# Four more single steps, in half products over 64 rows, at the head of a fused MLP's forward and backward pass

## The chip, the cores and the metric

The kernel runs on one core of a Trainium2 chip. The time is the device time of one execution in microseconds (us); the median of several executions is what is compared. The engines are named as in the profile: PE (matrix products), PEld (PE's weight loads), DVE (vector engine), ACT (scalar engine), POOL and SP (here they issue transfers for the most part). Each engine works through its own queue in order, and waits for the others through semaphores.

## The reference

One MLP layer with a GELU, forward and backward, in bfloat16, for 2048 rows, D = 448 and F = 1792:

```python
h   = gelu_tanh(x @ w1 + b1)          # 2048 x 1792
out = h @ w2 + b2                     # 2048 x 448
# vjp with grad_out g:
gh  = (g @ w2.T) * gelu_tanh'(x @ w1 + b1)
gx  = gh @ w1.T ;  gw1 = x.T @ gh ;  gb1 = sum(gh)
gw2 = h.T @ g   ;  gb2 = sum(g)
```

Six results are returned: out, gx, gw1, gb1, gw2, gb2. In the kernel u stands for x @ w1 (transposed, F on the partitions), q for g @ w2.T.

## The kernel before

**Tiles.** The 2048 rows are cut into four blocks of 512 (NB). F is cut into 14 tiles of 128, taken two at a time: a *step* k is one block and one pair of F tiles, so there are 28 steps (NSTEP), seven to a block. For a step PE makes u (into two banks of PSUM, the accumulator memory) and q (into a two-bank tile). D = 448 is three times 128 and a rest of 64, so each of the two F tiles needs three products over 128 rows and a *tail* over 64 rows.

**Full and half products.** A product over 128 rows can also be made as two *half products* over 64 rows each, one on the lower and one on the upper rows of the array, side by side with another half product. `side_by_side(one, other)` issues such pairs: a low half of `one` with a high half of `other`. Each product goes into two banks in turn, so that no bank is written from both halves at once; `half_product` (L257) puts a wait of PE on itself where a bank changes its half. u of a step needs 6 pairs, q 6 pairs, and the tails of a u and a q go side by side (`pe_tail_pair`, `pe_tails`).

**Elementwise work of a step.** ACT copies u out of PSUM with its bias (`copy_u`, L346), squares it (`act_square`, L355), takes its gelu into hT (`act_gelu`, L352) and a tanh of a cubic that DVE prepares (`act_tanh`, L364). DVE makes the cubic (L383 and L385 for one step, L359 and L360 for two), the gate (L387 to L394, or L368 to L375), and last *gh*, the gradient (L400), which multiplies the gate with q out of PSUM and so frees q's bank. The areas are fixed: AZ for cubic and gate, U4 for the u of two steps.

**Units.** A *unit* is one output tile of 128 rows x 448: kind "o" is out = hT times w2, kind "x" is gx = ghT times w1T, each 14 products over the F tiles, or 28 half products. Two units go side by side (`units_side`): first one gets the low half of every F tile and the other the high half, then (second = True) the reverse. A finished unit is cast to bfloat16 by ACT (L441, kind "x" and the first block's "o") or by DVE (L443, the other "o"), and POOL issues its store. `evictions()` casts whatever is finished, at the place where it is called. The units come in the order o, x of block 0, o, x of block 1, and so on, four each.

**Single steps.** Steps 0 to 7 (NSINGLE = 8) run one by one: in step i, PE makes u of step f = i + 2 and q of step i, and between their sections pieces of units that fill the time in which a bank must not be touched. At the end of step i ACT has tanh i, the copies, square and gelu of f; DVE has one chain written out by name (`dve_chain`). The units of block 0's out run in steps 1 to 6, two x units in steps 6 and 7.

**Paired steps.** From then on two steps ks run together, with elementwise work over both: tanh over 2048 elements, a gate in five instructions with `evictions` in its midst, two gh. In the first three pairs (n <= 2) PE makes u in full products (`pe_u_fulls`, L242), in the first two also q (`pe_q_fulls`, L303) and one x unit each (`pieces`, L430). From the third pair on (k = 12 and 13) q and the next u are made side by side (`pe_q_rows`), and two o or x units run side by side in the midst of the next u.

**Banks.** Eight banks: four single (`one0` to `one3`) for u, and for units when free, and two double ones (`two0`, `two1`). A single step's q always uses `two0`; in pairs the even step uses `two0` and the odd one `two1`. `open_two(1, 2)` opens two units in `two1`. Single steps' u use `one0` and `one1`, pairs use all four.

**Order.** The program's order is each engine's order: nothing is reordered afterwards. `traffic(i)` issues, on SP, the transposed copies of gh and the loads of the next blocks' x and g; `stores(n, fmax)` issues n stores of h. After the 28 steps the rest of the units, and then gw1 and gw2 are made (from 154 us on in the profiled execution).

Of the kernel before, what the change touches and what calls it, by code (L numbers as in the profile page):

```python
# [11 lines left out]
BF16 = mybir.dt.bfloat16  # L12
# [7 lines left out]
def kernel(  # L20
# [15 lines left out]
    nc = tc.nc  # L36
    P = 128
# [9 lines left out]
    SPB = SB // P  # L47
    NPAIR = NF // 2
    NSTEP = NB * NPAIR
    NSINGLE = 8  # L50
    LEAD = 2
    NWAKE = 10
    STG = 5
# [140 lines left out]
    PU, PQ = {}, {}  # L194
    order_a, order_b = [0, 1, 2, 3], [0, 1]
    U4 = tmp.tile([P, 4, SB], BF16, name="U4", tag="U4", bufs=1)
    SETS = [8, 4]

    def cols(p, a):
        return slice((2 * FP[p] + a) * P, (2 * FP[p] + a + 1) * P)  # L200
# [4 lines left out]
    def place(first, ks):  # L205
        return AZ[:, first:first + 2 * len(ks), :]
# [4 lines left out]

    def part_z(ks):
        k = ks[0]
        return place(4 * (k % 3) + 2 if k < NSINGLE else 2 * (k % 2), ks)

    def runs(ks):
        out = []
# [88 lines left out]
    def side_by_side(one, other, part=slice(0, None)):  # L306
        for lo, hi in list(zip(one(LOW), other(HIGH)))[part]:
            half_product(*lo)
            half_product(*hi)
# [8 lines left out]
        return lambda hf: [(("q", k, a), PQ[k][:, a, :], w2T[hf, kt, cols(p, a)], gT[b][hf, kt, :], hf, False, last and kt == KF)  # L318
                           for kt in range(1, KF + 1)]

    def unit_of(un, first, tiles):
        src, w = (hT, w2_sb) if un.kind == "o" else (ghT, w1T_sb)
        return lambda hf: [(un, un.ps, src[un.b][hf, t, un.j * P:(un.j + 1) * P], w[hf, 2 * FP[t // 2] + t % 2, :], hf,
                            first and t == 0, not first and t == NF - 1 and not un.b2_pe) for t in tiles]

    def b2_of(un):
        return lambda hf: [(un, un.ps, row0[hf, :], b2_bc[hf, :], hf, False, hf.start == (0 if un.j % 2 else DL))]

    def units_side(uns, second, tiles=range(NF)):
        one, other = uns[::-1] if second else uns  # L330
        side_by_side(unit_of(one, not second, tiles), unit_of(other, not second, tiles))
        if second and tiles[-1] == NF - 1:
            if one.b2_pe:
                side_by_side(b2_of(one), b2_of(other))
            for un in uns:
                un.done = NPAIR
                open_units.remove(un)
                finished.append(un)
# [77 lines left out]

    class Unit:
        def __init__(self, kind, b, j):
            self.kind, self.b, self.j, self.done, self.ps = kind, b, j, 0, None
            self.b2_pe = kind == "o" and b == 0  # L420
            self.by_act = kind == "x" or self.b2_pe

# [4 lines left out]
        def emit(self, p):  # L427
            src, w = (hT, w2_sb) if self.kind == "o" else (ghT, w1T_sb)
            for a in range(2):
                nc.tensor.matmul(self.ps, lhsT=src[self.b][:, 2 * p + a, self.j * P:(self.j + 1) * P],  # L430
                                 rhs=w[:, 2 * FP[p] + a, :], start=(p == 0 and a == 0),
                                 stop=(p == NPAIR - 1 and a == 1 and not self.b2_pe), skip_group_check=True)
            if p == NPAIR - 1 and self.b2_pe:
                nc.tensor.matmul(self.ps, lhsT=row0[:], rhs=b2_bc[:], start=False, stop=True, skip_group_check=True)
            self.done += 1

        def evict(self):
            st = stg.tile([P, SB], BF16, name="st", tag="st")
# [36 lines left out]
    def evictions(most=NS):  # L475
        for un in finished[:most]:
            un.evict()
        del finished[:most]
# [6 lines left out]
    def stores(n, fmax):  # L485
        for _ in range(n):
            if stored[0] <= fmax:
                store_h(stored[0])
                stored[0] += 1

    def traffic(i):
        for t in turns.get(i, []):
            turn_gh(*t)
        if i in loads:
            kind, b = loads[i]
            (load_x if kind == "x" else load_g)(b)
        if i == 6:
            other_halves()
# [17 lines left out]
    uns = [open_units[0:2], open_units[2:4]]  # L516
    pieces(4, 0, -1)

    def tiles(p):
        return range(2 * p, 2 * p + 2)  # L520

# [9 lines left out]
    for i in range(1, NSINGLE):  # L531
        f = i + LEAD
        if i < 6:
            between = [(uns[1], False, tiles(i)), (uns[0], True, tiles(i)[:1]), (uns[0], True, tiles(i)[1:]), (uns[1], True, tiles(i))]
        elif i == 6:
            between = [(uns[0], True, tiles(i)), (uns[1], False, tiles(i)[:1]), (uns[1], False, tiles(i)[1:]), (uns[1], True, tiles(i))]
        else:
            between = [(uns[0], False, range(6, 10)), (uns[0], False, range(10, 12)), (uns[0], False, range(12, 14)), (uns[0], True, range(0, 6))]
        open_u(f)
        open_q(i)  # L540
        side_by_side(u_of(f, 0, True), u_of(f, 1, True))
        units_side(*between[0])
        side_by_side(u_of(f, 1), u_of(f, 0))
        units_side(*between[1])
        pe_tail_pair(f, i, 1)
        pe_tail_pair(f, i, 0)
        units_side(*between[2])
        side_by_side(q_of(i, 0), q_of(i, 1))
        units_side(*between[3])
        side_by_side(q_of(i, 1, True), q_of(i, 0, True))  # L550
        if i < 6:
            units_side(uns[0], False, tiles(i + 1))
        if i > 1:
            act_tanh([i])
        evictions(2)
        copy_u(f, "aa")
        evictions()
        act_square([f])
        act_gelu([f])
        if i == 1:  # L560
            dve_chain("both 1", "cubic 2", "gate 1", "cubic*u 2", "slope 2", "gh 1", "slope*h 2", "cubic 3")
        elif i < 7:
            dve_chain(f"both {i}", f"cubic*u {i + 1}", f"gate {i}", f"slope {i + 1}", f"gh {i}", f"slope*h {i + 1}", f"cubic {f}")
        else:
            dve_chain("both 7", "cubic*u 8", "gate 7", "cubic 9", "gh 7", "cubic*u 9")
        if i == 6:
            open_two(1, 2)
            uns = [open_units[-2:]]
            units_side(uns[0], False, range(0, 6))
        if i == 7:  # L570
            units_side(uns[0], True, range(6, NF))
        traffic(i)
        if i >= 6:
            stores(2, f - 1)

    g_swap = {}
    g_low = const.tile([P, SB], BF16, name="g_low")
    nq = NSTEP // 2 - NSINGLE // 2

    def two_units(banks):  # L580
        for n in banks:
            open_unit(one_bank(n, "ps")[:, 0:D])
        return open_units[-2:]

    def pe_q_rows(ks, nxt):
        k0, k1 = ks
# [6 lines left out]
        side_by_side(q_of(k0, 1, True), q_of(k0, 0, True))  # L593

    for n in range(nq):
        i = NSINGLE + n
        k = NSINGLE + 2 * n
        ks = [k, k + 1]
        fs = [k + 2, k + 3] if k + 2 < NSTEP else []
        nxt = [k + 4, k + 5] if n >= 2 and k + 4 < NSTEP else []  # L600
        if n == 0:
            evictions()
        act_tanh(ks)
        dve_gate(ks, evictions)
        if n <= 2:
            for f in fs:
                pe_u_fulls(f)
        if n < 2:
            pe_tails(fs, ks)
            for q in ks:  # L610
                pe_q_fulls(q)
            for f in fs:
                copy_u(f, "aa")
            for q in ks:
                dve_gh(q)
            open_one()
            pieces(28, k + 1, k - 1)
            act_square(fs)
            act_gelu(fs)
            evictions(1)  # L620
            dve_cubic(fs)
        else:
            if fs:
                pe_tails(fs[::-1], ks[::-1])
            for f in fs[::-1]:
                copy_u(f, "aa")
            pe_q_rows(ks, nxt)
            for q in ks[::-1]:
                dve_gh(q)
            if nxt:  # L630
                open_u(nxt[0])
                side_by_side(u_of(nxt[0], 0, True), u_of(nxt[0], 1, True), slice(0, 1))
                open_two(1, 2)
                uns = open_units[-2:]
                units_side(uns, False)
                side_by_side(u_of(nxt[0], 0, True), u_of(nxt[0], 1, True), slice(1, None))
                units_side(uns, True)
                side_by_side(u_of(nxt[1], 1), u_of(nxt[1], 0))
                side_by_side(u_of(nxt[0], 1), u_of(nxt[0], 0))
            elif fs:  # L640
                uns, held = two_units(order_a[2:4]), two_units(order_a[0:2])
                units_side(uns, False)
                units_side(held, False)
                pe_tails([], [k + 2, k + 3])
                units_side(uns, True)
            if fs:
                act_square(fs)
                act_gelu(fs)
                dve_cubic(fs)
        if i == 8:  # L650
            nc.gpsimd.dma_start(out=g_low[0:DL, :], in_=gT[1][DL:P, 0, :])
            g_swap[1] = g_low
        if i == 15:
            nc.gpsimd.dma_start(out=g_low[DL:P, :], in_=gT[3][0:DL, 0, :])
            g_swap[3] = g_low
        traffic(i)
        stores(3, k + 1)
# [164 lines left out]
```

## Time and profile before

| | us |
|---|---|
| median of 3 executions | 269.21 (268.45 to 270.72) |
| the profiled execution | 268.56 |
| its span | 266.8 |
| PE busy in the span | 261.6 (98%) |
| DVE busy | 173.4 (65%) |
| ACT busy | 138.7 (52%) |
| PE's share of the chain that ended last | 94% |

The span is the profiled stretch; the execution's own time is 1.8 us longer. Busy times of PE are modelled ends of pipelined products: two half products side by side both count once. A *start* in the timeline is a more exact figure than a length, since an instruction's length holds its pipeline too; the step from one start to the next is what an instruction costs its queue.

### The profile page before, as it was taken

How to read it: one execution, taken by the hardware profiler on the slowest of the kernel's cores; microseconds unless marked ns; L12 is line 12 of the kernel's file. 1: busy time of each engine (PE TensorE's matmuls, PEld its weight loads, DVE VectorE, ACT ScalarE, POOL GpSimd, SP SyncE). 2: the span in 40 equal slices, each digit the busy share in tenths (PEclk: the TensorE clock that was granted, in tenths of full speed). 3: DMA queues.
4: the chain of work that ended last, by engine and by line, in shares of the span. 5: the costliest groups of instructions: out<-in, count | busy, mean ns of one | idle time of the engine just before them, and what ended most of it. 6: DMA issues, size and time to landing. Idle time of an engine off the chain costs nothing.

```text
span 266.8 us, 5001 instructions
## 1 busy us (share of the span) xinstructions
PE 261.6 (98%) x2082; PEld 159.9 (60%) x2082; DVE 173.4 (65%) x202; ACT 138.7 (52%) x162; POOL 40.3 (15%) x52
## 2 busy tenths in 40 slices
PE   7999999999999999999999999999999999999995
PEld 3367888744446565555658888864444765555554
DVE  2699997799998979669897731129999990000000
ACT  2899998899986686878659410022111111121111
POOL 1001004101002021010301020220700008900000
PEclk9999999999999999999999999999999999999999
DMA  7999999999999966264361359999511102999961
GB/s 160 252 227 211 175 213 188 288 232 206 259 225 257 220 172 170 54 164 94 111 157 43 72 120 256 357 197 230 138 39 39 52 20 58 200 225 225 161 163 34
DMA packets 111734, 44.46 MB, mean 167 GB/s; under 512 B 91040, under 2 KB 110576, under 8 KB 111712
## 3 DMA queue, kind: packets, MB, share of 16 engines
q1 hardware_dynamic: 104608, 36.14, 65.2%
q10 hardware_dynamic: 5248, 3.71, 5.6%
q0 software_dynamic: 1856, 4.30, 5.3%
q8 instruction: 16, 0.26, 0.4%
q14 instruction: 6, 0.05, 0.1%
HBM read 7.23 MB, written 14.23 MB: 80 GB/s over the span
## 4 chain that ended last, share of the span: by engine, by line
PE 94%; ACT 2%; DMA 2%; DVE 0%; issue 0%; ACTq 0%
PE ps L263 29%; PE ps_v L774 16%; PE ps_w L742 14%; PE pq L263 13%; PE pu L263 12%; PE pu L242 4%; PE ps_w L753 2%; PE pq L303 2%; PE ps L430 2%; DMA xT<-in_x_dram 2%; ACT AZ L355 1%; ACT hT L352 1%; DVE U L348 0%; ACT U L346 0%; ACT AZ L364 0%
## 5 line engine op out<-in xcount | busy, mean ns | idle before, releaser
L263 PE MATMUL ps<-w_sb,hT 64*128 64x448 bf16 x432 | 50.7, 349 | 0.3 <-ACT hT L352 0.3
L263 PE MATMUL pq<-gT,w2T 64*128 64x512 bf16 x338 | 49.9, 376 | 0.0
L774 PE MATMUL ps_v<-g_nat,h_nat 128*128 128x448 bf16 (+1 forms) x240 | 42.6, 340 | 0.0
L400 DVE SCALAR_TENSOR_TENSOR ghT<-AZ,pq 128x1024 bf16<-128x1024 bf16 x28 | 33.9, 1220 | 12.8 <-PE pq L263 11.8
L346 ACT ACTIVATE U<-pu,b1T 128x512 bf16<-128x512 f32 x54 | 33.3, 686 | 17.0 <-PE pu L263 12.7
L263 PE MATMUL ps<-w1T_sb,ghT 64*128 64x448 bf16 x392 | 40.8, 349 | 0.0
L444 POOL DMA_DIRECT2D out_dram<-st x32 | 18.9, 595 | 137.2 <-ACT st L441 84.0
L263 PEld LDWEIGHTS <-hT 64*128 64x128 bf16 x432 | 29.3, 94 | 13.7 <-ACT hT L352 0.8
L742 PE MATMUL ps_w<-gh_nat,x_nat 128*128 128x512 bf16 (+1 forms) x192 | 36.5, 352 | 0.0
L774 PEld LDWEIGHTS <-h_nat 128*128 128x128 bf16 x240 | 23.3, 98 | 19.3 <-DMA out_dram<-st 0.3
L263 PEld LDWEIGHTS <-ghT 64*128 64x128 bf16 x392 | 28.7, 94 | 9.2
L263 PE MATMUL pu<-xT,w_f 64*128 64x512 bf16 x228 | 33.1, 376 | 0.0
L263 PEld LDWEIGHTS <-w2T 64*128 64x128 bf16 x344 | 26.3, 94 | 9.5 <-PE pq L263 0.4
L364 ACT ACTIVATE AZ<-AZ 128x2048 bf16<-128x2048 bf16 (+1 forms) x18 | 27.5, 1526 | 7.4 <-DVE AZ L360 7.3
L728 DVE TENSOR_TENSOR acc<-acc,gh_nat 128x1792 f32<-128x1792 f32 x14 | 30.0, 2142 | 0.5
L742 PEld LDWEIGHTS <-x_nat 128*128 128x128 bf16 x192 | 18.7, 98 | 17.9 <-issue 0.4
L355 ACT ACTIVATE AZ<-U 128x1024 bf16<-128x1024 bf16 (+1 forms) x19 | 27.7, 1460 | 0.8 <-DVE U L348 0.4
L352 ACT ACTIVATE hT<-U 128x1024 bf16<-128x1024 bf16 (+1 forms) x20 | 27.6, 1383 | 0.0
L441 ACT CAST st<-ps 128x448 bf16<-128x448 f32 x20 | 9.8, 531 | 30.9 <-PE ps L263 28.7
L777 ACT CAST st<-ps_v 128x448 bf16<-128x448 f32 (+1 forms) x15 | 7.6, 507 | 34.8 <-PE ps_v L774 34.8
L745 ACT CAST st<-ps_w 128x512 bf16<-128x512 f32 (+1 forms) x12 | 6.4, 532 | 27.2 <-PE ps_w L742 27.2
L263 PEld LDWEIGHTS <-w_f 64*128 64x128 bf16 x228 | 15.6, 94 | 7.9 <-issue 0.2
(60 smaller groups left out, 214.2 us busy)
## 6 DMA issues: line engine op xcount, KB each, us to landing
hT_dram<-hT SPq DMA_DIRECT2D x28, 256.0 KB, 3.0
out_dram<-st POOLq DMA_DIRECT2D x32, 112.0 KB, 3.6
x_nat<-in_x_dram SPq DMA_DIRECT2D x1, 1792.0 KB, 10.7
g_nat<-in_grad_out_dram SPq DMA_DIRECT2D x1, 1792.0 KB, 16.3
out_dram<-st ACTq DMA_DIRECT2D x13, 112.0 KB, 3.6
out_dram<-st ACTq DMA_DIRECT2D x9, 128.0 KB, 1.9
w_f<-in_w_dram SPq DMA_DIRECT2D x5, 192.0 KB, 4.4
w_sb<-in_w_dram SPq DMA_DIRECT2D x4, 224.0 KB, 3.7
```

What stands on the lines that cost most here:

```text
L242: nc.tensor.matmul(PU[f][a][:, rs], lhsT=w1_f[:, kt, cols(p, a)], rhs=xT[b][:, kt, rs], start=(kt == 0 and rs.start == 0), stop=False, ski ...
L263: mm = nc.tensor.matmul(ps, lhsT=w, rhs=m, start=start, stop=stop, tile_position=(hf.start, 0), skip_group_check=True)
L346: nc.scalar.activation(out=dst, in_=PU[f][a][:], func=ACT.Identity, bias=bias)
L352: nc.scalar.activation(out=rows(hT, r), in_=part_u(r), func=ACT.Gelu_apprx_tanh)
L355: nc.scalar.activation(out=part_a(ks), in_=part_u(ks), func=ACT.Square, scale=math.sqrt(3.0 * GELU_A * GELU_C))
L364: nc.scalar.activation(out=z, in_=z, func=ACT.Tanh, scale=-1.0 / 3.0)
L400: nc.vector.scalar_tensor_tensor(out=rows(ghT, [k]), in0=part_z([k]), scalar=1.0, in1=PQ[k][:], op0=ALU.subtract if single else ALU.add, o ...
L441: nc.scalar.copy(out=st[:, 0:D], in_=self.ps)
L444: nc.gpsimd.dma_start(out=(out2 if self.kind == "o" else gx2)[r:r + P, :], in_=st[:, 0:D])
L728: nc.vector.tensor_tensor(out=v, in0=in0, in1=gh_nat[:, b, :, j, :], op=ALU.add)
L742: nc.tensor.matmul(ps[:, 0:n * P], lhsT=x_nat[:, st_, kt * P:(kt + 1) * P], rhs=gh_nat[:, b, ft0:ft0 + n, j, :], start=(st_ == 0), stop=(s ...
L774: nc.tensor.matmul(ps[:, 0:w], lhsT=h_nat[ft][:, st_, :], rhs=g_nat[:, st_, h * w:(h + 1) * w], start=(st_ == 0), stop=(st_ == NS - 1))
```

## The change

NSINGLE goes from 8 to 12: steps 8 to 11, which ran as two pairs with full products, now run as single steps with half products. What hangs on it:

- Steps 7 to 11 have the same form. Their 50 filling places (10 to a step, two after each section of u, after the tails, and after each section of q) are taken by four x units of block 0, two by two: `ahead` (the two opened in step 6) and `later` (two more, in banks `one2` and `one3`, opened in step 7). All four units end in step 11, where the `evictions()` behind copy_u casts them: `later` first, then `ahead`. Before, two were cast at the first pair and one at each of the next two.
- The first pair (n = 0) is now k = 12 and 13 and makes u of 14 and 15 with `pe_u_rows`, 12 half-product pairs; everything from there on is as before from the third pair on. `pe_u_fulls` is left for the start alone.
- The single steps' DVE chain goes on to step 10 in the form of steps 2 to 6; step 11 has the chain that step 7 had ("both 11", "cubic*u 12", "gate 11", "cubic 13", "gh 11", "cubic*u 13").
- A unit's first and last product are now told by a count (`slots`) and no longer by the F tile, so that a unit's tiles can come in any order.
- The areas in AZ for pairs move (SETS, `part_z`). The copy to g_low, which the first swapped tails need, is issued at the end of step 9 (before: after the first pair). `traffic` runs at steps 9 and 11 with the numbers of the old first two pairs; h stores stay three to two steps.

On the engines' queues PE gets 88 products more (88 full ones become 176 half ones), ACT 6 instructions more, DVE 12 more.

```diff
-    NSINGLE = 8
+    NSINGLE = 12
...
-    SETS = [8, 4]
+    SETS = [0, 8]
...
+    def fill(part):
+        if isinstance(part, tuple):
+            part = [(part[0], part[1], t) for t in part[2]]
+        for uns, second, t in part:
+            units_side(uns, second, [t])
...
         else:
-            between = [(uns[0], False, range(6, 10)), (uns[0], False, range(10, 12)), (uns[0], False, range(12, 14)), (uns[0], True, range(0, 6))]
+            if i == 7:
+                ahead, later = xs, two_units((2, 3))
+                slots = [(ahead, False, t) for t in range(6, NF)] + [(later, False, t) for t in range(NF)]
+                slots += [(ahead, True, t) for t in range(NPAIR)] + [(later, True, t) for t in range(NF)]
+                slots += [(ahead, True, t) for t in range(NPAIR, NF)]
+            between = [slots[2 * c:2 * c + 2] for c in range(5)]
+            del slots[0:10]
...
         if i < 6:
             units_side(uns[0], False, tiles(i + 1))
+        elif i > 6:
+            fill(between[4])
         if i > 1:
             act_tanh([i])
-        evictions(2)
+        if i == 6:
+            evictions(2)
         copy_u(f, "aa")
         evictions()
         act_square([f])
         act_gelu([f])
...
-        elif i < 7:
+        elif i < NSINGLE - 1:
             dve_chain(f"both {i}", f"cubic*u {i + 1}", f"gate {i}", f"slope {i + 1}", f"gh {i}", f"slope*h {i + 1}", f"cubic {f}")
         else:
-            dve_chain("both 7", "cubic*u 8", "gate 7", "cubic 9", "gh 7", "cubic*u 9")
+            dve_chain(f"both {i}", f"cubic*u {i + 1}", f"gate {i}", f"cubic {f}", f"gh {i}", f"cubic*u {f}")
...
-        if i == 7:
-            units_side(uns[0], True, range(6, NF))
-        traffic(i)
+        if i == 9:
+            nc.gpsimd.dma_start(out=g_low[0:DL, :], in_=gT[1][DL:P, 0, :])
+            g_swap[1] = g_low
+        if i < 8 or i % 2:
+            traffic(i if i < 8 else (i + 7) // 2)
         if i >= 6:
-            stores(2, f - 1)
+            stores(1 if i > 7 and i % 2 else 2, f - 1)
...
+    def pe_u_rows(fs):
+        for f in fs:
+            open_u(f)
+            side_by_side(u_of(f, 0, True), u_of(f, 1, True))
+        for f in fs:
+            side_by_side(u_of(f, 1), u_of(f, 0))
...
     for n in range(nq):
-        i = NSINGLE + n
+        i = 10 + n
...
         act_tanh(ks)
         dve_gate(ks, evictions)
-        if n <= 2:
-            for f in fs:
-                pe_u_fulls(f)
-        if n < 2:
-            pe_tails(fs, ks)
-            for q in ks:
-                pe_q_fulls(q)
-            ...
-            open_one()
-            pieces(28, k + 1, k - 1)
-            ...
+        if n == 0:
+            pe_u_rows(fs)
+        if fs:
+            pe_tails(fs if n == 0 else fs[::-1], ks[::-1])
+        for f in fs[::-1]:
+            copy_u(f, "aa")
+        pe_q_rows(ks, nxt)
+        for q in ks[::-1]:
+            dve_gh(q)
```

## The prediction

> **What bounds the kernel now.** I read the engine totals first, then PE's waits, then the timelines of PE, ACT and DVE around the part that is changed. Totals of the page (busy us, share of the span, instructions):
>
> ```profile
> PE 261.6 (98%) x2082; PEld 159.9 (60%) x2082; DVE 173.4 (65%) x202; ACT 138.7 (52%) x162; POOL 40.3 (15%) x52
> ```
>
> PE's waits, all of them (us in total, times, longest):
>
> ```profile
> PE pw L188 <- DVE AZ L142: 1.2, 1, 1.2
> PE pu L242 <- DMA xT<-in_x_dram: 0.4, 1, 0.4
> PE ps L263 <- ACT hT L352: 0.3, 1, 0.3
> ```
>
> After 14.1 us PE never waits for another engine, and the chain that ended last is PE for 94%. So a change can gain only what lies between products, and loses every new wait in full. PE's timeline (start, length, instruction) where the paired steps of the first blocks run:
>
> ```profile
> 48.53 0.91 PE L263 MATMUL pq<-gT,w2T 64*128 64x512 bf16 x6
> 49.18 1.77 PE L263 MATMUL ps<-w1T_sb,ghT 64*128 64x448 bf16 x16
> 50.89 2.76 PE L242 MATMUL pu<-xT,w_f 128*128 128x512 bf16 x12
> ...
> 54.55 2.76 PE L303 MATMUL pq<-gT,w2T 128*128 128x512 bf16 x12
> 57.15 2.81 PE L430 MATMUL ps<-w1T_sb,ghT 128*128 128x448 bf16 x14
> 59.80 2.75 PE L242 MATMUL pu<-xT,w_f 128*128 128x512 bf16 x12
> ...
> 72.26 2.11 PE L263 MATMUL pq<-gT,w2T 64*128 64x512 bf16 x18
> 74.21 0.81 PE L263 MATMUL pu<-xT,w_f 64*128 64x512 bf16 x6
> ...
> 75.72 2.81 PE L263 MATMUL ps<-w_sb,hT 64*128 64x448 bf16 x28
> ```
>
> The prices follow from starts. 18 half products over 512 columns take 74.21 - 72.26 = 1.95, so a side-by-side pair takes 0.217 us; the 28 over 448 columns last until 78.36, the next start, so such a pair takes 0.189. Full products take the same: 12 in 2.60 (54.55 to 57.15) is 0.217, 14 in 2.65 is 0.189. A change of form costs something: 16 half products from 49.18 should end at 50.69, but the next starts at 50.89.
>
> **What is removed.** Full products, and with them seven changes of form. The stretch from step 7's first product (43.51) to the first units of pair 12/13 (75.72) lasts 32.21 us. Its work at the prices above, in the new order, is five single steps of 14 pairs over 512 columns and 10 over 448, 14 x 0.217 + 10 x 0.189 = 4.92 each, so 24.60, and then 32 pairs over 512: 12 (u 14, 15), 4 (tails), 9 (q), 3 (u 17), 3 (q), 1 (u 16), 6.94 us. Together 31.54. The same products lie in the old stretch (u 9 to 15, q 7 to 13, 50 unit pairs), so the form changes cost 0.67 us, and that is **the whole gain** on PE.
>
> The 88 full products become 176 half products. In the rows above that is free, because a pair takes what one full product takes. The Trainium skill, "TensorEngine Tiling (Array Packing)", section Performance Considerations, gives about 60 cycles of overhead to each matmul; as an estimate from that page, 88 more would be some 2.2 us at the 2.4 GHz it is clocked at, and the sum would be 273.7. The rows price that overhead at nothing for products of this width.
>
> **What the single steps need beside PE.** A single step cost ACT 4.24 us (copies at 31.26 and 35.79, less 0.29 of waiting) and DVE 4.39 (its "both" at 31.00 and 35.54, less 0.15). Both are under 4.92, so steps 7 to 11 should run without a wait; without that margin (in steps of 4.53 DVE had 0.15 left) each would cost DVE's excess. ACT gets 6 more instructions and DVE 12, of half the width; they lie in that margin. The stores of h stay three to two steps, the turned copies and loads keep their pair, and the copy to g_low stands at the end of step 9 instead of the first pair: on SP and POOL these are the same transfers in nearly the same places, no product waited for one after 14.1 us, and g_low is used at the end of step 11, two steps (9.8 us) after its issue against 3.0 us to landing. I take all of this as nothing; a late g_low would cost its lateness.
>
> **What is added: a queue at the seam.** Before, the units of the last single step were cast behind gelu, on ACT (start, length, instruction):
>
> ```profile
> 47.87 1.06 ACT L355 ACTIVATE AZ<-U 128x1024 bf16<-128x1024 bf16 x1
> 48.83 1.04 ACT L352 ACTIVATE hT<-U 128x1024 bf16<-128x1024 bf16 x1
> 50.99 0.97 ACT L441 CAST st<-ps 128x448 bf16<-128x448 f32 x2 [1.12 <-PE ps L263]
> 51.84 1.92 ACT L364 ACTIVATE AZ<-AZ 128x2048 bf16<-128x2048 bf16 x1
> ```
>
> Now all four x units end inside step 11, and its `evictions()` stands between copy_u and act_square: the third cast waits for the last product of the step, and behind it on ACT stand the square of 13, gelu and tanh of 12 and 13. On DVE the "cubic 13" waits for that square, and behind it stands "gh 11", which frees the bank of q 12. Call E the end of step 11's products (43.51 + 24.60 = 68.11). DVE's rows at the old seam price the chain:
>
> ```profile
> 48.96 0.43 DVE L383 TENSOR_SCALAR AZ<-AZ 128x1024 bf16<-128x1024 bf16 x1 [1.19 <-ACT AZ L355]
> 49.48 1.22 DVE L400 SCALAR_TENSOR_TENSOR ghT<-AZ,pq 128x1024 bf16<-128x1024 bf16 x1
> 50.62 0.68 DVE L385 TENSOR_TENSOR AZ<-AZ,U 128x1024 bf16<-128x1024 bf16 x1
> 51.22 0.69 DVE L368 TENSOR_SCALAR AZ<-AZ 128x2048 bf16<-128x2048 bf16 x1
> 52.01 1.23 DVE L370 TENSOR_TENSOR AZ<-AZ,hT 128x2048 bf16<-128x2048 bf16 x1
> 53.27 0.69 DVE L371 TENSOR_SCALAR AZ<-AZ 128x2048 bf16<-128x2048 bf16 x1
> 53.88 0.69 DVE L374 TENSOR_SCALAR AZ<-AZ 128x2048 bf16<-128x2048 bf16 x1
> ```
>
> Third cast at E + 0.30 (50.99 against the old 50.69); two casts 0.85, so square 13 at E + 1.15; cubic 1.09 later (47.87 to 48.96), E + 2.24; gh 11 at 2.76; cubic*u at 3.90; the gate's four at 4.50, 5.29, 6.55 and 7.16; its product at 7.88 (0.72, as 53.88 to 54.60); gh 13 1.33 after that (63.93 to 65.26), E + 9.21; the units of the freed bank 1.29 later (74.42 to 75.72 and 85.87 to 87.15), **E + 10.50**. PE alone would be there at E + 6.94, so it stands 3.56 us. I expect this in three pieces: about 0.95 before q 12's tails (gh 11 ends at E + 3.98, PE is there at 3.03); about 1.4 before u 17 (tanh from 4.62, copies from 6.54, the second of 15 ready at 7.83, PE there at 6.41); 1.1 to 1.3 before the units. The old seam did not show this: 7.1 us after its cubic, DVE's gh (56.06) still had 0.23 us to wait for PE, which had full products to do until then.
>
> From the units on, gh stands to PE as in every later pair (1.28 to 1.30), so nothing more is lost or won back. **Sum:** 68.11 + 10.50 = 78.61 against 75.72, +2.89 (or 3.56 lost, 0.67 gained). On the profiled execution's 268.56 that is 271.45, which I give as 271.5. That execution lies 0.65 under the median of 269.21; on the median it would be 272.1. The unknown is how well seven start-to-start steps add up in a place where they never ran together: none of the seam's 3.56 lost is the lower end, all of it and one pair's 1.2 us of DVE slack the upper; I take the sum, since each row is the same instruction at the same width.
>
> **Rivals.** (1) *PE covers the seam*: faster, 268.56 - 0.67 = 267.9. It decides from gh 13 starting before E + 6.3, where the 0.67 is used up. For it: the old seam was covered. Against: ACT's built order has the four casts ahead of the square. 0.04. (2) *Part of the chain lies beside something*: gh 11 or the copies come some 1 to 1.5 us earlier, 270.2. For it: PE has 6.94 us of other products in the seam. Against: the instructions are serial on DVE. 0.16. (3) *The lateness lives on* into pair 14/15, whose gh had 1.20 us to spare: 272.7. Against: gh to units is as before. 0.13. (4) *PE's clock falls in the gaps.* The ten wake-up products took 4.19 us (L188) where ten at 0.217 take 2.17: one such stretch again costs 2.0 us, so 273.5. Against: the pieces are at most 1.4 us with products between, and the granted clock is 9 in all 40 slices. 0.07. The Trainium skill, "TensorE: Matmul & The Clock Gate", section Part 1, has the clock halved after an idle window of about 3.4 us; the trace has no such gap after the start, so it cannot confirm it. The forecast itself has 0.60.
>
> **How the numbers follow.** 1% is 2.7 us, about what a measurement of this kernel can tell from no change. The forecast's own spread of some 0.3 puts two thirds of its 0.60 above that: with (3) and (4) 0.58 to 0.60 for slower by over 1%; I say 0.58. Within 1%: the rest of the forecast and (2), 0.38. Faster: only (1), and 0.67 us is under 1%, so 0.04 holds what I have not seen. The range 270.1 to 273.2 takes in (2) and (3), and leaves out (1) and most of (4).
>
> **What would show it.** Right: no full products between 43.5 and 76; steps 7 to 11 of 4.92 us; then PE idle for gh (DVE), copies (ACT) and gh again, 3 to 4 us in sum, before the first w_sb units of pair 12/13, whose start moves from 75.7 to 78.6, and everything behind it by as much. Wrong: those units before 76.5, idle PE in steps 8 to 10, a granted clock under 1.0 behind the seam, or waits in pair 14/15.

## The result, and the profile after

The changed kernel takes 271.95 us (median of six, 271.10 to 273.13) against 268.83 us (median of six, 268.20 to 272.82) for the kernel before: **1.2% slower**, ratio 1.0120 with a 95% interval of 1.0089 to 1.0151. The profiled execution took 272.67 us, of which the span is 270.9; the profiled execution before took 268.56 and 266.8. The ratios here leave out executions that lie over 1.5% above the fastest of their kernel; two profiles shown below are of such executions, and only the stretches named are read from them.

The page's totals of the kernel after (busy us, share of the span, instructions):

```profile
PE 262.0 (97%) x2170; PEld 164.3 (61%) x2170; DVE 173.1 (64%) x212; ACT 139.3 (51%) x168; POOL 40.2 (15%) x52
```

PE has 88 instructions more (88 full products became 176 half ones), and its busy time grew by 0.4 us only, while the span grew by 4.1. So the time went into waits. PE's five longest waits in the kernel after (what is waited for, us in total, times, longest):

```profile
PE pq L263 <- DMA gT<-in_grad_out_dram: 1.5, 1, 1.5
PE pw L188 <- DVE AZ L142: 1.2, 1, 1.2
PE ps L263 <- DVE ghT L402: 1.1, 1, 1.1
PE pu L263 <- ACT U L348: 0.8, 2, 0.6
PE pq L263 <- DVE ghT L402: 0.4, 1, 0.4
```

The second was there before, as were two short ones early in the run that are left out here; the other four are new. Three of them (gh, the copies of u, gh again) are at the seam and were forecast; the first, on a load of the gradient, was not. PE's timeline of the kernel after, from step 7 to the first units of pair 12/13 (start, length, instruction, in brackets the wait ahead of it):

```profile
43.17 0.91 PE L263 MATMUL pu<-xT,w_f 64*128 64x512 bf16 x6
...
47.10 0.39 PE L263 MATMUL pq<-gT,w2T 64*128 64x512 bf16 x1 [1.51 <-DMA gT<-in_grad_out_dram]
...
59.66 0.95 PE L263 MATMUL pu<-xT,w_f 64*128 64x512 bf16 x6
...
64.57 0.95 PE L263 MATMUL pu<-xT,w_f 64*128 64x512 bf16 x6
...
69.48 2.90 PE L263 MATMUL pu<-xT,w_f 64*128 64x512 bf16 x24
...
73.39 0.37 PE L263 MATMUL pq<-g_low,w2T 64*128 64x512 bf16 x1 [0.36 <-DVE ghT L402]
...
76.51 0.37 PE L263 MATMUL pu<-xT,w_f 64*128 64x512 bf16 x1 [0.59 <-ACT U L348]
...
79.84 2.82 PE L263 MATMUL ps<-w_sb,hT 64*128 64x448 bf16 x28 [1.09 <-DVE ghT L402]
```

The steps start at 59.66, 64.57 and 69.48: 4.91 us each (4.92 forecast), all in half products, with no wait inside. E, the end of step 11's products, is 69.48. PE alone needs 6.94 us from there to the units, and takes 79.84 - 69.48 = 10.36 (10.50 forecast), so 3.42 are lost. By starts (which add up to 3.44 with the rounding) the loss is 0.89 before the tails of q 12 (73.39 against 72.50 by the prices), 1.11 around u 17 and 1.44 before the units; the profile's waits name less of it, because single products get through between the waits.

Where the whole span's 4.1 us went, in order of time: step 7 starts 0.34 us earlier (43.17 against 43.51); steps 7 to 11 take 26.31, which is 1.75 over the 24.56 that they take in the profile of run 1, with the same products and no wait (43.89 to 68.45), and that is the late load; the seam takes 10.36; the rest of the run takes 270.9 - 79.84 = 191.06 against 266.8 - 75.72 = 191.08. Nothing is lost or won back behind the units.

ACT's timeline of the kernel after shows the queue that makes the seam's loss:

```profile
68.41 0.96 ACT L444 CAST st<-ps 128x448 bf16<-128x448 f32 x2
69.83 0.97 ACT L444 CAST st<-ps 128x448 bf16<-128x448 f32 x2 [0.46 <-PE ps L263]
70.68 1.07 ACT L357 ACTIVATE AZ<-U 128x1024 bf16<-128x1024 bf16 x1
71.64 1.06 ACT L354 ACTIVATE hT<-U 128x1024 bf16<-128x1024 bf16 x1
73.97 1.91 ACT L366 ACTIVATE AZ<-AZ 128x2048 bf16<-128x2048 bf16 x1 [1.28 <-DVE AZ L387]
```

The last two casts wait 0.46 us for the step's last products, and the square of 13 (L357) can only start behind them, at E + 1.20 (1.15 forecast). DVE's timeline of the kernel after carries it on:

```profile
71.78 0.43 DVE L385 TENSOR_SCALAR AZ<-AZ 128x1024 bf16<-128x1024 bf16 x1 [3.27 <-ACT AZ L357]
72.12 1.22 DVE L402 SCALAR_TENSOR_TENSOR ghT<-AZ,pq 128x1024 bf16<-128x1024 bf16 x1
73.25 0.68 DVE L387 TENSOR_TENSOR AZ<-AZ,U 128x1024 bf16<-128x1024 bf16 x1
73.86 0.69 DVE L370 TENSOR_SCALAR AZ<-AZ 128x2048 bf16<-128x2048 bf16 x1
...
78.57 2.35 DVE L402 SCALAR_TENSOR_TENSOR ghT<-AZ,pq 128x1024 bf16<-128x1024 bf16 x2
...
90.00 2.52 DVE L402 SCALAR_TENSOR_TENSOR ghT<-AZ,pq 128x1024 bf16<-128x1024 bf16 x2 [1.20 <-PE pq L263]
```

DVE stands 3.27 us for that square, with gh 11 (72.12) queued behind cubic 13 (71.78), though the products that gh 11 needs end with the step (run 2 shows it start there). From gh 11 to gh 13 pass 6.45 us, exactly the 2.76 to 9.21 of the forecast. The next pair's gh (90.00) waits 1.20 us for PE, as in DVE's timeline of the kernel before:

```profile
85.87 2.52 DVE L400 SCALAR_TENSOR_TENSOR ghT<-AZ,pq 128x1024 bf16<-128x1024 bf16 x2 [1.20 <-PE pq L263]
```

The slack is whole, and the lateness ends at the units.

The new wait at the front of the stretch comes from the queue of SP. First the kernel before, then the kernel after, each in SP's timeline (start and length of the issue on the queue):

```profile
39.23 2.57 SPq L114 DMA_TRANSPOSE gT<-in_grad_out_dram  x1
```

```profile
39.86 2.83 SPq L114 DMA_TRANSPOSE gT<-in_grad_out_dram  x1
```

PE's timeline of the kernel before has the first product that needs this load:

```profile
46.04 0.38 PE L263 MATMUL pq<-gT,w2T 64*128 64x512 bf16 x1
```

In the kernel before, the load landed 6.6 us after its issue, at 45.8, and PE asked for it at 46.04, which is 2.53 after step 7's start: a margin of 0.2 us. The new step 7 puts four pairs of units, not six, ahead of its tails, so PE asks 2.15 us after the start, at 45.32, and here the load landed only at 47.06, 7.2 us after an issue that was itself 0.63 later. The new order accounts for 0.38 us of the wait: in the old order PE would have asked at 43.17 + 2.53 = 45.70, and would still have stood 1.36 us. The rest is how the load came in this one execution.

### The profile page after: what moved, and what is told of

The parts are those of the page before. It is cut to its first block, busy times and chain, and to the rows that moved or that the text cites. A ratio compares the mean times of both kernels' runs of the same rounds, so it can differ in the third digit from the quotient of the medians.

```text
span 270.9 us, 5197 instructions
## 1 busy us (share of the span) xinstructions
PE 262.0 (97%) x2170; PEld 164.3 (61%) x2170; DVE 173.1 (64%) x212; ACT 139.3 (51%) x168; POOL 40.2 (15%) x52
## 4 chain that ended last, share of the span: by engine, by line
PE 78%; SPq 14%; DMA 3%; issue 1%; ACT 1%; DVE 1%
PE ps L263 27%; PE ps_v L783 16%; PE ps_w L751 13%; PE pq L263 11%; PE pu L263 9%; SPq L135 3%; SPq L183 3%; DMA gT<-in_grad_out_dram 3%; PE ps_w L762 2%; SPq L114 1%; SPq L104 1%; SPq L131 1%; SPq L121 1%; DVE ghT L402 1%; SPq L171 1%
## 5 line engine op out<-in xcount | busy, mean ns | idle before, releaser
L263 PE MATMUL pq<-gT,w2T 64*128 64x512 bf16 x386 | 58.4, 376 | 1.5 <-DMA gT<-in_grad_out_dram 1.5
L263 PE MATMUL ps<-w1T_sb,ghT 64*128 64x448 bf16 x448 | 52.5, 349 | 0.0
L263 PE MATMUL pu<-xT,w_f 64*128 64x512 bf16 x300 | 44.3, 376 | 0.8 <-ACT U L348 0.8
L263 PEld LDWEIGHTS <-ghT 64*128 64x128 bf16 x448 | 33.3, 94 | 11.5
L263 PEld LDWEIGHTS <-w2T 64*128 64x128 bf16 x392 | 29.7, 94 | 14.0 <-DMA gT<-in_grad_out_dram 2.0
L366 ACT ACTIVATE AZ<-AZ 128x1024 bf16<-128x1024 bf16 (+1 forms) x20 | 27.8, 1390 | 8.6 <-DVE AZ L362 7.3
L357 ACT ACTIVATE AZ<-U 128x1024 bf16<-128x1024 bf16 (+1 forms) x21 | 28.2, 1342 | 0.9 <-DVE U L350 0.4
L263 PEld LDWEIGHTS <-w_f 64*128 64x128 bf16 x300 | 21.1, 94 | 11.3 <-issue 1.6
```

The source lines that it names most:

```text
L263: mm = nc.tensor.matmul(ps, lhsT=w, rhs=m, start=start, stop=stop, tile_position=(hf.start, 0), skip_group_check=True)
L357: nc.scalar.activation(out=part_a(ks), in_=part_u(ks), func=ACT.Square, scale=math.sqrt(3.0 * GELU_A * GELU_C))
L366: nc.scalar.activation(out=z, in_=z, func=ACT.Tanh, scale=-1.0 / 3.0)
```

## The experiments

Theory: most of the seam's 3.4 us comes from two pieces of order in step 11, the last two casts ahead of the square of 13 on ACT and cubic 13 ahead of gh 11 on DVE. Rivals: the load of the gradient alone makes the loss and the seam would be covered anyway; the half form of the products costs time itself. Each kernel was timed beside the kernel before on its chip, and the ratio is to that. The seam is given as the time from E to the units (10.36 in the kernel after, 6.94 for PE alone).

**1. The last two casts behind gelu.** The two casts that wait for the step's last products are left to the next place where casts are put, behind gelu 13.

```diff
-        evictions()
+        evictions(2 if i == NSINGLE - 1 else NS)
         act_square([f])
```

> Only two casts (later) stand ahead of the square of 13, the other two (ahead) come behind its gelu; all else as in the changed kernel. Seam theory (casts, square 13, cubic 13, gh 11 and the gate stand in one queue that ends at gh 13): the square starts at the end of step 11 minus 0.1 instead of plus 1.2, gh 13 and the units behind it come 1.2 us earlier, so 271.95 becomes 270.7, and the wait of PE for gh before q 12's tails is gone. Rival (the loss is the late g of block 1 at step 7 and the seam is hidden by later slack): the same time as the changed kernel, 271.5 to 272.5. A wait for g at step 7 should be there as in the changed kernel, if that is its rule: some 0.5 to 1.7 us.

Measured: 270.25 us (269.53 to 270.43) against 268.67, ratio 1.0053 (1.0036 to 1.0070). DVE's timeline of this kernel:

```profile
69.33 0.43 DVE L385 TENSOR_SCALAR AZ<-AZ 128x1024 bf16<-128x1024 bf16 x1 [1.85 <-ACT AZ L357]
69.67 1.22 DVE L402 SCALAR_TENSOR_TENSOR ghT<-AZ,pq 128x1024 bf16<-128x1024 bf16 x1
```

Cubic 13 waits 1.85 us instead of 3.27, and starts 0.88 after this kernel's E of 68.45 instead of 2.30. The units follow at 77.39, E + 8.94: two casts moved win 1.42 us of the seam.

**2. gh 11 ahead of cubic 13.** The same two instructions of DVE, in the other order.

```diff
-            dve_chain(..., f"gate {i}", f"cubic {f}", f"gh {i}", f"cubic*u {f}")
+            dve_chain(..., f"gate {i}", f"gh {i}", f"cubic {f}", f"cubic*u {f}")
```

> In step 11's chain on DVE gh 11 stands ahead of cubic 13; casts as in the changed kernel. Seam theory: gh 11 runs 0.0 instead of 2.6 us after the end of step 11, cubic 13 still waits for the square (2.3 after it), so cubic*u 13 and all behind it come 1.1 us earlier: units 9.2 us after the end of step 11 instead of 10.4, time 270.8. Rival (what is late is ACT's tanh and the copies behind it, not DVE): under 0.3 us gained, 271.7 or more.

Measured: 270.14 us (269.97 to 270.33) against 268.67, ratio 1.0055 (1.0038 to 1.0072). DVE's timeline of this kernel:

```profile
67.76 1.22 DVE L402 SCALAR_TENSOR_TENSOR ghT<-AZ,pq 128x1024 bf16<-128x1024 bf16 x1 [0.93 <-PE pq L263]
...
70.10 0.43 DVE L385 TENSOR_SCALAR AZ<-AZ 128x1024 bf16<-128x1024 bf16 x1 [1.11 <-ACT AZ L357]
```

gh 11 now uses time in which DVE stood, and starts 0.05 us before E (67.81). Units at 77.15, E + 9.34: 1.02 us won. Cubic 13 is where it was, at E + 2.29, so this is a gain of another kind than that of the first run.

**3. Both edits.**

> Both edits: two casts ahead of the square, and gh 11 ahead of cubic 13. Seam theory: units 8.0 us after the end of step 11, so 2.3 us gained, 269.6, still about 0.8 us over the kernel before; the form changes' gain of 0.67 is then more than half of what the seam takes. If the two edits free the same wait, the gain is that of one alone, 270.7 to 270.9.

Measured: 269.54 us (268.61 to 270.92, twelve executions) against 268.67, ratio 1.0030 (1.0008 to 1.0052). PE's timeline of this kernel:

```profile
68.63 2.85 PE L263 MATMUL pu<-xT,w_f 64*128 64x512 bf16 x24
...
76.73 2.83 PE L263 MATMUL ps<-w_sb,hT 64*128 64x448 bf16 x28 [0.76 <-DVE ghT L402]
```

E + 8.10, so 2.26 of the seam's 3.42 are gone, about the sum of the two (1.42 + 1.02). The order of four instructions in one step makes most of the slowdown. That is against the rivals: neither the form of the products nor the loads were touched.

**4. Step 7's tails later.** The fills of step 7 are 4, 4, 1, 1, 0 pairs of units instead of 2 each, so that PE asks for the gradient 0.76 us later than in the kernel after, and 0.38 later than in the kernel before.

```diff
-            between = [slots[2 * c:2 * c + 2] for c in range(5)]
-            del slots[0:10]
+            between = []
+            for c in ((4, 4, 1, 1, 0) if i == 7 else (2, 2, 2, 2, 2)):
+                between.append(slots[0:c])
+                del slots[0:c]
```

> Step 7 has 4, 4, 1, 1 and 0 unit pairs in its five filling places instead of 2 each, so that its tails, the first products with the g of block 1, come 0.76 us later; PE's work is the same. If the wait for g at step 7 (1.5 us in the changed kernel's profile) is there in every execution because the tails moved ahead by 0.38 us, the time falls by 0.4 to 0.76 us, to 271.2 to 271.6. If it was that one execution's, nothing changes, 271.95.

Measured: 271.49 us (271.24 to 272.44) against 268.67, ratio 1.0107 (1.0087 to 1.0126). The profile has no wait for the gradient, and the seam is as long as in the kernel after (68.19 to 78.41, 10.22). So the slowdown is there without the late load, and the rival of the load alone falls.

**5. A dose: two more casts ahead of the square.** Two of the step's results are cast a second time, into a tile that nothing reads.

```diff
+        again = finished[2:4] if i == NSINGLE - 1 else []
         evictions()
+        for un in again:
+            nc.scalar.copy(out=dose[:, 0:D], in_=un.ps)
         act_square([f])
```

> The changed kernel with two more casts on ACT ahead of the square of 13 (the two units of ahead are cast a second time, into a tile that nobody reads; the result stays as it is). Seam theory: two casts cost ACT 0.85 us from start to start, everything from the square to gh 13 is one queue, so the units behind the seam come 0.85 us later, 11.2 us after the end of step 11 instead of 10.4, and the time is 272.8. Rival (PE's stall has some other length, set by something that ACT's casts do not move): 271.95.

Measured: 273.32 us (272.88 to 277.69) against 269.08, ratio 1.0159 (1.0135 to 1.0182). ACT's timeline (this profile is of an execution with a late gradient load; only this stretch is read; lines are one higher than in the kernel after):

```profile
73.82 0.97 ACT L445 CAST st<-ps 128x448 bf16<-128x448 f32 x2 [0.46 <-PE ps L264]
74.67 1.12 ACT L587 CAST dose<-ps 128x448 bf16<-128x448 f32 x2
75.68 1.06 ACT L358 ACTIVATE AZ<-U 128x1024 bf16<-128x1024 bf16 x1
```

The dose takes 1.01 us from start to start (0.85 expected), the granted clock in this stretch is 1.00, the units come at E + 11.37 (10.36 + 1.01), and the ratio is 0.39% above that of the kernel after, some 1.05 us. The intervals overlap from 1.0135 to 1.0151, so by time alone the step is only likely; by the trace the two casts more are paid in full.

**6. u of steps 8 to 11 in full products.** This puts back half of the old form: one change to full and one back in each of four steps.

```diff
+        if i > 7:
+            pe_u_fulls(f)
+            open_q(i)
+            fill(between[0])
+        else:
             open_u(f)
             open_q(i)
             side_by_side(u_of(f, 0, True), u_of(f, 1, True))
             ...
```

> The changed kernel with u of steps 10 to 13 (made in steps 8 to 11) in full products again, six to a step, all else in half products: each of the four steps has one change from half to full and one back. By the rows before (0.20 from half to full, 0.09 back) a step takes 0.29 us longer, 5.21 us instead of 4.92, and the time grows by 1.2 us to 273.1. If the form changes cost nothing and the 0.67 us of the forecast came from elsewhere, 271.95.

Measured: 272.55 us (272.23 to 277.47) against 269.08, ratio 1.0129 (1.0109 to 1.0150). PE's timeline of this kernel:

```profile
53.80 1.47 PE L242 MATMUL pu<-xT,w_f 128*128 128x512 bf16 x6
...
58.92 1.47 PE L242 MATMUL pu<-xT,w_f 128*128 128x512 bf16 x5
...
64.05 1.47 PE L242 MATMUL pu<-xT,w_f 128*128 128x512 bf16 x6
```

A step takes 5.12 us instead of 4.91: two changes of form cost 0.21 us, where I had expected 0.29 (steps of 5.21), read from the first pair of changes in the kernel before. Over four steps that is 0.85. By time the kernel isn't told apart from the kernel after (1.0120); the profile agrees with the gain that the prediction gave to the form (0.67 for three such pairs, as shown below). The rival that half products cost time falls: a step with its u in halves is shorter than one with it in fulls.

**7. The same queue in the kernel before.** There the last units of step 7 are moved ahead of its end and their casts put between the copy of u and the square of 9; the products, their form and the rest of the schedule stay.

```diff
+        if i == 7:
+            units_side(uns[0], True, range(6, NF))
         if i > 1:
             act_tanh([i])
-        evictions(2)
+        if i == 6:
+            evictions(2)
         copy_u(f, "aa")
         evictions()
         act_square([f])
...
-        if i == 7:
-            units_side(uns[0], True, range(6, NF))
```

> The kernel before with one part of the change alone: at step 7 its two casts stand between copy_u and the square of 9, as at the new seam, instead of behind gelu. Products and their order are the same. Seam theory: the square moves from 47.9 to 51.8 us, cubic 9, gh 7 and the gate of 8 and 9 with it; the paired steps with full products are no longer than DVE's own work for them (gh to gh 9.2 us, PE 8.9), so the lateness is not made good there and appears in front of the units of pair 12/13: 3 to 4.3 us, time 272 to 273. Rival (the cover of the full products hides it): 268.7.

Measured: 272.47 us (272.03 to 276.53) against 269.08, ratio 1.0129 (1.0107 to 1.0151). ACT's timeline of this kernel, and then DVE's:

```profile
51.13 0.97 ACT L441 CAST st<-ps 128x448 bf16<-128x448 f32 x2 [3.15 <-PE ps L263]
51.98 1.07 ACT L355 ACTIVATE AZ<-U 128x1024 bf16<-128x1024 bf16 x1
```

```profile
53.09 0.43 DVE L383 TENSOR_SCALAR AZ<-AZ 128x1024 bf16<-128x1024 bf16 x1 [5.18 <-ACT AZ L355]
```

Without any new half product, the casts ahead of the square hold cubic 9 for 5.18 us (1.19 before), and the units of pair 12/13 start at 79.34 instead of 75.72; 0.14 of these 3.62 us were there at step 7's start (43.65 against 43.51). One edit of that order gives the old kernel a slowdown of the new one's size. This is the plainest case for the theory.

**8. The seam mended.** Together: gh 11 first, no casts ahead of the square in step 11 (the units of the second set end and are cast in step 10), the fills of step 11 as 1, 1, 1, 1, 6 and those of step 7 as in run 4.

```diff
-                slots += [(ahead, True, t) for t in range(NPAIR)] + [(later, True, t) for t in range(NF)]
-                slots += [(ahead, True, t) for t in range(NPAIR, NF)]
+                slots += [(later, True, t) for t in range(NF)] + [(ahead, True, t) for t in range(NF)]
...
+            for c in ((4, 4, 1, 1, 0) if i == 7 else (1, 1, 1, 1, 6) if i == NSINGLE - 1 else (2, 2, 2, 2, 2)):
...
-        evictions()
+        evictions(0 if i == NSINGLE - 1 else NS)
         act_square([f])
...
```

> The changed kernel with its seam mended: later's units end in step 10 and are cast there, ahead's are cast behind gelu 13, gh 11 stands ahead of cubic 13, step 11 has six of its ten filling pairs behind q (so that gh 11 can run 0.8 us earlier), and step 7 has the places of 4, 4, 1, 1, 0. Seam theory: gh 11 0.9 us before the end of step 11, gh 13 6.0 after it, the units 7.3 after it, against 6.9 for PE alone; 3.1 us of the seam are won back, and the rest of the form changes' 0.67 is left over: 268.4 to 268.9, within what can be told from the kernel before.

Measured: 269.40 us (268.88 to 273.30, twelve executions) against 269.08, ratio 1.0012 (0.9997 to 1.0027). The seam is 7.96 (68.67 to 76.63), not the 7.3 expected. DVE's timeline of this kernel has the reason:

```profile
66.43 0.69 DVE L394 TENSOR_SCALAR AZ<-AZ 128x2048 bf16<-128x2048 bf16 x1 [0.78 <-ACT AZ L366]
```

The casts, now in step 10, stand ahead of the tanh of 11 on ACT, and DVE waits 0.78 us for that tanh. A queue was moved, not removed.

**9. The kernel after again, and 10. the load of the gradient earlier.** The second brings the load of block 1's gradient ahead of the two of w1T on SP's queue, and takes the units of the second set first in step 7.

```diff
+    load_g(1)
     for t0, t1 in ((0, 8), (8, NF)):
         nc.sync.dma_start_transpose(out=w1T_sb[:, t0:t1, :], in_=w1[:, t0 * P:t1 * P])
-    load_g(1)
...
-                slots = [(ahead, False, t) for t in range(6, NF)] + [(later, False, t) for t in range(NF)]
+                slots = [(later, False, t) for t in range(6)] + [(ahead, False, t) for t in range(6, NF)]
+                slots += [(later, False, t) for t in range(6, NF)]
```

> The changed kernel once more, beside the next two on one chip, as their reference. By the first comparison 1.2% over the kernel before. A late g of block 1 at step 7 (1.5 us of waiting in the first profile, nothing to 0.2 in four of the later ones with the same step 7) should be seen again in some executions only.

> The changed kernel with the load of g of block 1 ahead of the two transposed loads of w1 on SP's queue, and the first six filling places of step 7 given to later's first tiles, whose w1 lands first. If the late g is a regular part of the loss, PE never waits for g and the time falls by 0.3 to 0.7 us against the changed kernel beside it; if it is rare, the two agree within 0.2%. Where w1's second half comes too late instead, PE's waits name it.

Measured: the kernel after 272.47 us (271.75 to 276.76) against 268.83, ratio 1.0122 (1.0094 to 1.0149); with the earlier load 271.58 us (271.32 to 271.88), ratio 1.0098 (1.0073 to 1.0124), no wait for the gradient and a seam of 10.30 (68.45 to 78.75). With the load out of the way the change costs 2.75 us (271.58 - 268.83). The difference to the kernel after, 0.24%, lies inside the intervals: that the late load costs something in every execution is not shown. Of the seven profiles with the new order of step 7 (the kernel after and runs 1, 2, 3, 5, 6 and 9), four have no wait for this load or one of at most 0.3 us, one has 1.5 and two have 3.4. What it can cost is seen in the profiled execution of run 9, which took 276.76 us. PE's timeline there:

```profile
49.49 0.39 PE L263 MATMUL pq<-gT,w2T 64*128 64x512 bf16 x1 [3.42 <-DMA gT<-in_grad_out_dram]
```

The load landed 8.5 us after its issue, at 49.47, and PE stood for 3.42 us. The old order, 0.38 us later at its first use, would still have stood for about 3.0; whether the clock would then have fallen as shown below is open.

**11. Mended again.** As run 8, with the earlier load, with the fills of step 7 at 2 each again, and with the second set's casts behind the tanh of 11, which stands ahead of the copy of u in step 11.

```diff
...
-        if i == 6:
+        if i in (6, NSINGLE - 1):
             evictions(2)
         copy_u(f, "aa")
-        evictions()
+        evictions(0 if i >= NSINGLE - 2 else NS)
         act_square([f])
...
```

> The mended seam with the casts of later behind tanh 11 in step 11 instead of in step 10 (where they held back tanh 11, and with it DVE's both 11, by 0.8 us), and with g of block 1 loaded earlier. Seam theory: gh 11 0.8 us before the end of step 11, the units 7.4 us after it (8.0 in the first mended version, 10.4 in the changed kernel, 6.9 for PE alone), time 0.4 to 0.6 us under the first mended version: 0.998 to 1.000 of the kernel before.

Measured: 268.55 us (268.13 to 270.46, twelve executions) against 268.83, ratio 0.9989 (0.9971 to 1.0007). PE's timeline of this kernel:

```profile
68.06 2.75 PE L263 MATMUL pu<-xT,w_f 64*128 64x512 bf16 x24
...
75.32 2.83 PE L263 MATMUL ps<-w_sb,hT 64*128 64x448 bf16 x28 [0.19 <-DVE ghT L402]
```

The seam is 7.26, with one wait of 0.19 us for gh left, and the units start at 75.32, 0.40 ahead of the kernel before. Of that, 0.21 was there at step 7's start (43.30 against 43.51); the stretch itself is 0.19 shorter, because the steps take 24.76 with these fills (24.56 in run 1) and the seam keeps 0.32 over PE's own 6.94. The forecast gain of the form, 0.67, would put the ratio at 0.9975; the interval holds that and no change, so it isn't told apart from the kernel before. No version here beats it beyond its interval.

## Why the prediction was right

- **The time.** 271.5 forecast, 271.95 measured; +2.89 forecast on the profiled execution, +2.75 measured where the load is out of the way, +3.12 between the medians of the kernel itself. The profiled execution alone came out at 272.67, 4.11 over the profiled execution before, of which 1.75 is the late load.
- **What is removed.** Right as a sum: without the late load the five steps take 24.56 (24.60 forecast). The count was wrong: the old stretch has six changes of form, three to full products and three back, not seven. PE's timeline of the kernel before has the rows that start behind four of them (those at 50.89 and 54.55 stand in the prediction):

```profile
53.58 0.39 PE L263 MATMUL pu<-xT,wt 64*128 64x512 bf16 x1
...
62.49 0.39 PE L263 MATMUL pu<-xT,wt 64*128 64x512 bf16 x1
...
63.46 2.76 PE L303 MATMUL pq<-gT,w2T 128*128 128x512 bf16 x12
...
71.39 0.39 PE L263 MATMUL pu<-xT,wt 64*128 64x512 bf16 x1
```

At the prices of the prediction the change at 50.89 costs 0.20 us and each of the other five 0.09 to 0.10, which together is the whole 0.67. A pair of changes is thus 0.22 in the mean, and run 6 measures 0.21; the 0.29 expected there was the first and dearest pair. Why that one is dearer is open. The 176 half products cost nothing beyond their columns: steps of 4.91 us are what the columns alone give. So the trace does not bear out the sum of 273.7 by the overhead of about 60 cycles for each matmul (the Trainium skill, "TensorEngine Tiling (Array Packing)", Performance Considerations). The Trainium skill goes on there to say that a matmul with a free dimension of 1 takes as long as one with 60; read as a floor of that kind, the overhead would not show in products of 448 and 512 columns, and it does not show here.
- **What the single steps need beside PE.** Right: no wait of PE on ACT or DVE in steps 7 to 11. By the page's totals DVE got 10 instructions more (202 to 212), not 12.
- **The queue at the seam.** Right, mechanism and size: 10.36 against 10.50, in three pieces of 0.89, 1.11 and 1.44 against 0.95, 1.4 and 1.1 to 1.3. The second piece was forecast 0.3 too long and the third 0.1 to 0.3 too short, so it is partly luck that the sum is this close. Runs 1 and 2 shorten the loss by its two pieces of order, run 5 lengthens it, run 7 makes the loss in the kernel before, run 11 takes all but 0.32 us of it away.
- **The step that failed.** "on SP and POOL these are the same transfers in nearly the same places ... I take all of this as nothing." The transfers did stay, but the first reader of one moved 0.38 us up, against a load with 0.2 us of margin. The change's own share of the wait is thus at most 0.38 us an execution. The profiled execution waited 1.5 us and one of run 9's 3.42, most of which is a load that came late there. Runs 4 and 10, where the wait is gone, lie 0.13 to 0.24% under the kernel after, which their intervals do not settle. The forecast looked at whether each load kept its place in the queue, not at when its data were first asked for, nor at how far a landing can vary.
- **The rivals.** (1) fell: gh 13 starts at 78.57, E + 9.09, far behind E + 6.3, and the units at 79.84. (2) fell: gh 11 to gh 13 is serial, 6.45. (3) fell: the next gh has its 1.20 us again. (4) fell at the seam, where the granted clock is 1.00 (window 69.50 to 79.84), but is real for longer gaps, as below.

## What to carry to other kernels

Where an in-order engine passes from one kind of step to another, price its queue from end to end, by start-to-start times, and ask of each instruction whether something behind it was ready earlier: here two casts and one cubic, all needed, cost 2.3 of the seam's 3.4 us by their place alone (run 3), in a kernel whose DVE and ACT are busy 64% and 51% of the span. A cast that waits for PE's last product does not belong ahead of the operation that feeds PE's next bank. And where products are reordered, compare each load's landing with the new time of its first use, even if the load itself is not moved.

## What the runs showed of the hardware

A long gap of PE lowers its clock. Windows of run 9's profile (window, length, busy us and instructions of PE, PEld, DVE, ACT and POOL, granted PE clock, DMA share, GB/s):

```profile
45.70:49.20 3.50, 0.36 (x4) 0.00 (x0) 2.23 (x4) 0.26 (x1) 0.00 (x0) 1.00 1.21 263
49.20:50.70 1.50, 1.21 (x12) 0.55 (x14) 0.00 (x0) 0.75 (x2) 0.52 (x1) 0.89 1.42 116
50.70:52.70 2.00, 2.00 (x12) 0.85 (x10) 0.00 (x0) 1.97 (x3) 0.00 (x0) 0.50 0.89 69
52.70:54.70 2.00, 2.00 (x18) 0.91 (x15) 0.90 (x1) 1.49 (x2) 0.00 (x0) 0.73 0.98 68
54.70:60.00 5.30, 5.30 (x55) 3.72 (x53) 4.62 (x9) 3.39 (x5) 0.00 (x0) 1.00 1.09 260
```

After 3.42 us of standing, PE runs on at 1.00 for almost a microsecond; then the granted clock is 0.50 for about 3.4 us (by the rows, from 50.4 to 53.8), and full again. A late load of that length costs its lateness and then half of that stretch again: run 9's steps 7 to 11 take 29.92 us (43.64 to 73.56) instead of 24.56, of which 3.7 are PE's wait and 1.7 the slower clock. Run 5's profile shows the same behind a wait of 3.44 us, with a granted clock of 0.50 from 50.00 to 52.00. In the kernel after, the gap of 1.51 us and the shorter ones of the seam left it at 1.00. That agrees with the Trainium skill, "TensorE: Matmul & The Clock Gate", Part 1, which has the clock halved after an idle window of about 3.4 us; it was the fourth rival's mechanism, met at a place where I had not looked for it.

The second finding is how far a load's landing varies. In the eleven profiles that have this transposing load in the same place of SP's queue, it landed between 4.6 us (run 1) and 8.7 us (run 5) after its issue: 6.6 in the kernel before, 7.2 in the kernel after, 8.5 in run 9.
